# First block: rounding of the first piece of w_out begun ahead of the second front instead of behind it

## The chip, the cores and the metric

The kernel runs on one core of a Trainium2 chip. The metric is the device time of one execution in microseconds (us). A core has five engines that run side by side, each through its own list of instructions in order: TensorE (PE, matrix products; its weight loads are shown as PEld), VectorE (DVE), ScalarE (ACT), GpSimd (POOL) and SyncE (SP, which here only issues DMAs). They wait for each other through semaphores.

## The reference

The first half is a Fourier mixing: for x of 8 x 3008 x 256, the real part of a two-dimensional transform over the sequence and the feature axis. Its result, as 24064 rows of 256, goes through a two-layer network with a squared Relu between:

```python
def _attn_ref(x):
    X = np.fft.fft(x, axis=1)
    X = np.fft.fft(X, axis=2)
    return X.real.astype(np.float32)

def _moe_ref(x, w_in, w_out):
    h = x @ w_in
    r = np.maximum(h, 0.0)
    g = r * r
    return (g @ w_out).astype(np.float32)
```

`w_in` is 256 x 2048 and `w_out` is 2048 x 256. They arrive as 64-bit floats, since they are scaled by a 64-bit number, and are rounded to 32 bits in the kernel.

## The kernel before, in words

**The work.** The transform along the sequence is done as products with tables of cosines and sines (`dft_ops`, results `Pt`, `Qt` and a row `Et` for each of the 8 batches). The transform along the features is folded into the first layer's weights: `begin_win` multiplies each piece of `w_in` with the feature tables and gives `G1` and `G2`. So the first layer reads `Pt`, `Qt` with `G1`, `G2`.

**Steps.** Hidden features come in NJ = 8 pieces of 256 (two times 128). The columns of a batch come in blocks of up to 251. One step `i` is one piece `j` of one block of one batch. Its *front* (L822 to L840) makes on PE, for both halves, a product with `G1` (L832) and one with `G2` (L833), and on DVE a scaled sum with `Et` (L835), a sum (L837) and a difference (L838). `combine` (L845) puts Relu (L847) and Square (L848) on ACT. The *back* of a step (L863) multiplies with `w_out` and comes two steps later (LAG = 2); in the first block it is the plain form, sixteen matmul passes of L872. From the second block on `combine` also makes sums on POOL (L855 to L858), and the back is L885.

**The weights, in the first block.** The eight pieces of `w_in` and of `w_out` are loaded, rounded and used while the eight steps of the first block run. Rounding 64-bit words is `convert` (L263): DVE takes the exponent (L274) and the mantissa (L279) out of the high words, ACT turns the exponent into a 32-bit scale (L276, L277) and, in the shared form, scales the mantissa (L282). That is the first part, issued by the call itself. Later, `halves` puts the sign and the low words in on DVE (L285, L287), and `product` multiplies mantissa and scale, in the shared form on POOL (L292), else on DVE (L294). A load is two DMAs from SP (L259). `load_wout(j, shared)` (L326) is load and first part for a piece of `w_out`; `begin_win(j)` (L300) is the same for a piece of `w_in`, and keeps two more closures: `products` (L305: matmuls L309 with the feature tables, then two copies into `G1`, `G2` on ACT, L310) and `for_e` (L313: four small matmuls L318 with `G2`, then L320 on DVE into `gE`).

**The order.** The program is written out by hand: each engine does its instructions in the order in which the Python code issues them, with no scheduler. In the main loop (L1164), step `i` of the first block issues in this order: `multiply` (the POOL products put off so far), `front`, `weights()` (L1124), `combine`, the back of step i - 2, then `for_e` of the next piece, `leftover` (L1154: `halves` of what lies in `late`) and L320. In `weights()`, step `i` first issues the products of piece i + 1 of `w_in`. Step 0 then begins piece 3 of `w_in`, rounds piece 2 and takes `halves` of piece 3. Step i > 0 loads piece i - 1 of `w_out`, finishes rounding piece i + 2 of `w_in` (not in step 1) and begins piece i + 3 of `w_in`. Piece 0 of `w_out` is so begun in step 1, behind the second front, and read by the first back, in step 2.

The scratch tiles of the rounding rotate in pools: the exponents in two buffers (`fd`), the mantissas in three (`scratch`, L247), the loaded words over several pools (`load`, L251).

Of the kernel before, what the change touches and what calls it, by code (L numbers as in the profile page):

```python
# [82 lines left out]
def kernel(  # L83
# [20 lines left out]
    NJ = NFC // 2  # L104
# [126 lines left out]
    def pair_in(j):  # L231

        return moe_w_in.rearrange("(c p) (h j f) -> j c p h f", p=P, j=NJ, h=2)[j]

    def pair_out(j):

        return moe_w_out.rearrange("(c j p) (o e) -> j c p o e", j=NJ, p=P, o=1)[j]

    def parts(w, k):
        return w.rearrange("p c (e h) -> p h (c e)", h=k)  # L240
# [10 lines left out]
    def load(src):  # L251

        nonlocal raws
        pool, tag = (gp, "g") if raws in (1, 2) else (xp, "x") if raws % (NX + 1) else (ep, "c")
        raws += 1
        single = src.dtype == F32
        raw = pool.tile([P, 2, CH, 1 if single else 2], src.dtype if single else U32, name="raw", tag=tag)
        for c in range(2):
            nc.sync.dma_start(out=raw[:, c].rearrange("p (o e) w -> p o (e w)", o=src.shape[2]),  # L259
                              in_=src[c] if single else src[c].bitcast(U32))  # L260
        return raw

    def convert(dst, raw, shared=False):  # L263


        k = dst.shape[1]
        if raw.dtype == F32:
            return (lambda: None), (lambda: nc.vector.tensor_copy(dst, parts(raw[:, :, :, 0], k))), False
        low, high = raw[:, :, :, 0], raw[:, :, :, 1]
        m = scratch()  # L270
        e = fp.tile([P, 2, CH], F32, name="fd", tag="fd")
        mb, eb = m.bitcast(U32), e.bitcast(U32)

        nc.vector.tensor_scalar(out=eb, in0=high, scalar1=20, scalar2=0x7FF,  # L274
                                op0=ALU.logical_shift_right, op1=ALU.bitwise_and)
        act(e, eb, AF.Relu, bias=ramp[:, 0:1], scale=-1.0)  # L276
        act(eb, e, AF.Relu, bias=ramp[:, 1:2], scale=-2.0 ** 23)  # L277

        nc.vector.tensor_scalar(out=mb, in0=high, scalar1=0xFFFFF, scalar2=0x100000,  # L279
                                op0=ALU.bitwise_and, op1=ALU.bitwise_or)  # L280
        if shared:
            act(m, mb, AF.Copy, scale=2.0 ** -20)  # L282

        def halves():
            nc.vector.scalar_tensor_tensor(out=eb, in0=high, scalar=0x80000000, in1=eb,  # L285
                                           op0=ALU.bitwise_and, op1=ALU.bitwise_or)
            nc.vector.scalar_tensor_tensor(out=m, in0=low, scalar=2.0 ** (-52 if shared else -32),  # L287
                                           in1=m if shared else mb, op0=ALU.mult, op1=ALU.add)

        def product():  # L290
            if shared:
                nc.gpsimd.tensor_tensor(out=dst, in0=parts(m, k), in1=parts(e, k), op=ALU.mult)  # L292
            else:
                nc.vector.scalar_tensor_tensor(out=dst, in0=parts(m, k), scalar=2.0 ** -20, in1=parts(e, k),  # L294
                                               op0=ALU.mult, op1=ALU.mult)

        return halves, product, shared


    def begin_win(j, shared=False):  # L300

        w = ep.tile([P, 2, CH], F32, name="win", tag="sB" if j % 2 else "sA")
        finish = convert(parts(w, 1), win.pop(j, None) or load(pair_in(j)), shared)

        def products():  # L305
            for tab, G, nm in ((cosd, G1, "mC"), (sind, G2, "mD")):
                pg = psm.tile([P, CH], F32, name="pg", tag=nm)
                for i in range(2):
                    nc.tensor.matmul(pg, tab[:, i], w[:, i], start=i == 0, stop=i == 1)  # L309
                nc.scalar.copy(G.rearrange("p (h j f) -> j p h f", h=2, j=NJ)[j],  # L310
                               pg.rearrange("p (h f) -> p h f", h=2))

        def for_e():  # L313

            ps = psd.tile([P, CH], F32, name="pe", tag="d")
            for h in range(2):
                fc = j + NJ * h
                nc.tensor.matmul(ps[:, h:h + 1], G2[:, fc * P:(fc + 1) * P], last, start=True, stop=True)  # L318

            return lambda: nc.vector.tensor_scalar_mul(gE[:, j::NJ], ps[:, 0:2], 0.5)  # L320

        win[j] = finish, products, for_e
# [3 lines left out]
    def load_wout(j, shared):  # L326

        return convert(wout[:, j].rearrange("p h c e -> p h (c e)"), load(pair_out(j)), shared)
# [693 lines left out]
    def rounded(j):  # L1022
        halves, product, _ = win[j][0]
        halves()
        product()
# [93 lines left out]
            f()  # L1119
            spent, room = spent + t, room - t  # L1120

    late, products = [], []

    def weights():  # L1124


        if i + 1 < NJ:
            win[i + 1][1]()
        if i == 0:
            begin_win(3, True)  # L1130
            rounded(2)
            split(win[3][0])
        else:
            mine = [load_wout(k, i != NJ - 2 or k == i) for k in OUT.get(i, ())]
            if 1 < i < NJ - 2:
                rounded(i + 2)
            if i + 3 < NJ:
                begin_win(i + 3)
            for pair in mine:
                late.append(pair)  # L1140

    OUT = {i: (i - 1,) for i in range(1, NJ - 2)}
    OUT[NJ - 2] = NJ - 3, NJ - 2
    OUT[NJ - 1] = NJ - 1,

    def split(pair):
        halves, product, shared = pair
        halves()
        if shared:
            products.append(product)  # L1150
        else:
            product()
# [11 lines left out]
    for i in range(len(steps) + LAG + 4):  # L1164
        if i < len(steps):
            b, k0, n, j = steps[i]
            if i == NJ:
                for k in range(NX):
                    load_later(k)
            if NJ <= i < NJ + NL:  # L1170
                load_column(i - NJ)
            if i % per == 0:
                assert not side
                side = ahead(b + 1) if b + 1 < B else []
                spent, pace = 0.0, sum(t for t, _ in side) / sum(share(i + k) for k in range(per - 2))
            multiply()
            g = front(b, k0, n, j, between)
            if i < NJ:
                weights()
                s = combine(n, g, True)  # L1180
            elif i < 2 * NJ:
                if j < 4:
                    sum_wout(slice(j // 2 * (NJ // 2), (j // 2 + 1) * (NJ // 2)), j % 2)
# [79 lines left out]
```

## Time and profile before

| what | value |
|---|---|
| time, median of 3 runs | 1923.56 us (1923.0 to 1924.24) |
| the profiled execution's own time | 1921.07 us |
| its span, first to last instruction | 1919.3 us |
| mean granted PE clock | 0.999 |
| PE, busy share of the span | 99% |
| DVE, POOL, ACT | 75%, 58%, 50% |
| ACT in the first four fortieths of the span | 20%, 70%, 50%, 50% |
| share of the chain that ended last: PE, DVE | 96%, 3% |
| DMA, mean over the span | 36 GB/s (224 and 118 GB/s in the first two fortieths) |

The page is of one execution. A fortieth of the span is 48 us, so the preparation (tables, first transform) fills about the first, and the first block, with all the rounding of weights, most of the second. The "chain that ended last" follows back from the last instruction, at each step to what released it. A busy time of PE counts matmuls with modelled ends. An instruction's idle time before it is shown in brackets in the timeline, with the engine and line that ended it.

### The profile page before, as it was taken

What the parts mean: (1) busy time and instruction counts of PE and PEld (TensorE: products, weight loads), DVE (VectorE), ACT (ScalarE), POOL (GpSimd) and SP (SyncE); (2) the same over time, 40 slices, a digit from 0 to 9 for tenths busy, and PEclk for the clock granted to TensorE, in tenths of its full rate; (3) what the DMA queues carried; (4) which work ended last, traced back from release to release, by engine and by line L of the source; (5) the groups of instructions that cost most, each with busy time, mean ns of one, the idle gap of its engine ahead of it and who ended that gap; (6) DMA issues with size and microseconds to landing.
All of it is one profiled execution on the core that took longest, in us unless ns stands there. A gap on an engine that the chain in (4) does not pass through costs nothing.

```text
span 1919.3 us, 28162 instructions
## 1 busy us (share of the span) xinstructions
PE 1907.5 (99%) x9270; PEld 1700.7 (89%) x9270; DVE 1444.5 (75%) x3646; ACT 952.4 (50%) x1201; POOL 1120.8 (58%) x1709
## 2 busy tenths in 40 slices
PE   9999999999999999999999999999999999999998
PEld 7888898888988898888988889888898888988887
DVE  8988887787687876788668876788767777655554
ACT  2755554555454554445544454455544555444444
POOL 0255655665566665665566665556655665566565
PEclk9999999999999999999999999999999999999999
DMA  7331211110011101111011100111001101000100
GB/s 224 118 36 30 55 29 36 28 43 16 28 36 42 34 12 35 31 44 28 12 36 44 39 20 12 47 37 36 22 19 45 36 12 22 28 12 12 22 11 23
DMA packets 146622, 69.58 MB, mean 36 GB/s; under 512 B 130145, under 2 KB 137259, under 8 KB 146474
## 3 DMA queue, kind: packets, MB, share of 16 engines
q1 hardware_dynamic: 146022, 66.87, 13.8%
q8 instruction: 73, 1.20, 0.2%
q14 instruction: 75, 0.61, 0.1%
q0 software_dynamic: 176, 0.65, 0.1%
q10 hardware_dynamic: 276, 0.26, 0.0%
HBM read 43.03 MB, written 24.69 MB: 35 GB/s over the span
## 4 chain that ended last, share of the span: by engine, by line
PE 96%; DVE 3%; ACT 0%; DMA 0%; issue 0%; POOL 0%; DVEq 0%; ACTq 0%
PE ph L832 17%; PE ph L833 17%; PE mC L885 16%; PE mA L885 16%; PE mB L885 16%; PE mD L885 8%; PE pd L734 1%; PE pd L626 1%; PE mA L872 1%; PE mB L872 1%; PE pd L708 1%; DMA xt<-in_x_dram 0%; PE pg L309 0%; DVE w L509 0%; DVE fs L479 0%
## 5 line engine op out<-in xcount | busy, mean ns | idle before, releaser
L847 ACT ACTIVATE g<-g 128x1004 f32<-128x1004 f32 (+1 forms) x384 | 399.0, 1039 | 691.8 <-DVE g L838 438.1
L835 DVE SCALAR_TENSOR_TENSOR he<-Et,gE,ph 128x251 f32<-128x251 f32 (+1 forms) x768 | 362.7, 472 | 343.3 <-PE ph L833 338.9
L855 POOL TENSOR_TENSOR s<-g 128x251 f32<-128x251 f32 (+1 forms) x376 | 236.7, 629 | 636.7 <-ACT g L848 578.0
L832 PE MATMUL ph<-Pt,G 128*128 128x251 f32 (+1 forms) x1536 | 452.5, 376 | 0.0
L833 PE MATMUL ph<-Qt,G 127*128 127x251 f32 (+1 forms) x1536 | 451.4, 375 | 0.0
L848 ACT ACTIVATE g<-g 128x1004 f32<-128x1004 f32 (+1 forms) x384 | 399.3, 1040 | 12.2
L885 PE MATMUL mC<-s,wsum 128*128 128x251 f32 (+1 forms) x1504 | 381.5, 375 | 0.0
L885 PE MATMUL mA<-g,wout 128*128 128x251 f32 (+1 forms) x1504 | 380.2, 374 | 0.0
L837 DVE TENSOR_TENSOR g<-he,ph 128x251 f32<-128x251 f32 (+1 forms) x768 | 320.4, 417 | 53.5 <-POOL s L855 1.4
L833 PEld LDWEIGHTS ph<-Qt,G 127*128 127x128 f32 x1536 | 291.6, 190 | 35.4
L885 PEld LDWEIGHTS mC<-s,wsum 128*128 128x128 f32 x1504 | 285.8, 190 | 34.2
L832 PEld LDWEIGHTS ph<-Pt,G 128*128 128x128 f32 x1536 | 285.9, 189 | 33.5 <-DVE he L835 0.2
L838 DVE TENSOR_TENSOR g<-he,ph 128x251 f32<-128x251 f32 (+1 forms) x768 | 314.2, 409 | 0.0
L885 PEld LDWEIGHTS mA<-g,wout 128*128 128x128 f32 x1504 | 283.0, 189 | 34.9 <-issue 0.3
L856 POOL TENSOR_TENSOR s<-s,g 128x251 f32<-128x251 f32 (+1 forms) x376 | 270.7, 720 | 29.5
L857 POOL TENSOR_TENSOR s<-g 128x251 f32<-128x251 f32 (+1 forms) x376 | 272.3, 724 | 0.0
L858 POOL TENSOR_TENSOR s<-g,s 128x251 f32<-128x251 f32 (+1 forms) x376 | 241.8, 643 | 0.0
L885 PE MATMUL mB<-g,wsum 128*128 128x251 f32 (+1 forms) x752 | 220.5, 374 | 0.0
L885 PE MATMUL mD<-s,wout 128*128 128x251 f32 (+1 forms) x752 | 220.4, 374 | 0.0
L885 PE MATMUL mB<-s,wout 128*128 128x251 f32 (+1 forms) x752 | 220.0, 374 | 0.0
L885 PEld LDWEIGHTS mB<-g,wsum 128*128 128x128 f32 x752 | 142.8, 190 | 17.2
L885 PEld LDWEIGHTS mD<-s,wout 128*128 128x128 f32 x752 | 142.1, 189 | 17.5
(176 smaller groups left out, 1386.0 us busy)
## 6 DMA issues: line engine op xcount, KB each, us to landing
out_dram<-os SPq DMA_DIRECT2D x376, 56.0 KB
xt<-in_x_dram SPq DMA_DIRECT2D x39, 384.0 KB
xt<-in_x_dram SPq DMA_DIRECT2D x63, 128.0 KB
Et<-e_dram SPq DMA_DIRECT2D x7, 752.5 KB
out_dram<-os SPq DMA_DIRECT2D x288, 6.8 KB
raw<-in_moe_w_in_dram SPq DMA_DIRECT2D x16, 256.0 KB
raw<-in_moe_w_out_dram SPq DMA_DIRECT2D x16, 256.0 KB
xt<-in_x_dram SPq DMA_DIRECT2D x2, 512.0 KB
```

The lines of the kernel that those rows point to most:

```text
L832: nc.tensor.matmul(hP, G1[:, fs], pt[:, ks], start=True, stop=True)
L833: nc.tensor.matmul(hQ, G2[0:P - 1, fs], qt[0:P - 1, ks], start=True, stop=True)
L835: nc.vector.scalar_tensor_tensor(out=t, in0=et[:, ks], scalar=gE[:, fc:fc + 1], in1=hP, op0=ALU.mult, op1=ALU.add)
L837: tt(out=g[:, h, 0, 0:n], in0=t, in1=hQ, op=ALU.add)
L838: tt(out=g[:, h, 1, 0:n][:, ::-1], in0=t, in1=hQ, op=ALU.subtract)
L847: act(v, v, AF.Relu)
L848: act(v, v, AF.Square)
L855: gt(out=s1, in0=g21, in1=g22, op=ALU.add)
L856: gt(out=s2, in0=s1, in1=g11, op=ALU.subtract)
L857: gt(out=s3, in0=g11, in1=g21, op=ALU.subtract)
L858: gt(out=s4, in0=g12, in1=s2, op=ALU.subtract)
L885: nc.tensor.matmul(acc[nm][:, i, 0:n], w, v[:, 0:n], start=j == 0 and i == 0, stop=j == NJ - 1, skip_group_check=True)
```

## The change

`load_wout(0)` is called at the end of step 0's `weights()` instead of in step 1's. It is kept in `early`, and step 1 only moves it to `late`, so that its second part comes where it came before. Step 1 still begins piece 4 of `w_in` (there is no other load between the two, so the loads keep their order). The rest rewrites the same conditions: `OUT` begins at 2, and `1 < i` is implied.

```diff
-    late, products = [], []
+    early, late, products = [], [], []
...
             begin_win(3, True)
             rounded(2)
             split(win[3][0])
+            early.append(load_wout(0, True))
+        elif i == 1:
+            begin_win(4)
+            late.append(early.pop())
         else:
-            mine = [load_wout(k, i != NJ - 2 or k == i) for k in OUT.get(i, ())]
-            if 1 < i < NJ - 2:
+            mine = [load_wout(k, i != NJ - 2 or k == i) for k in OUT[i]]
+            if i < NJ - 2:
                 rounded(i + 2)
             if i + 3 < NJ:
                 begin_win(i + 3)
-            for pair in mine:
-                late.append(pair)
-
-    OUT = {i: (i - 1,) for i in range(1, NJ - 2)}
+            late.extend(mine)
+
+    OUT = {i: (i - 1,) for i in range(2, NJ - 2)}
     OUT[NJ - 2] = NJ - 3, NJ - 2
     OUT[NJ - 1] = NJ - 1,
```

On the engines, this puts L274 and L279 of piece 0 of `w_out` ahead of L320 and the second front on DVE, and L276, L277 and L282 of that piece ahead of Relu and Square of step 0 and the two copies L310 of piece 2 of `w_in` on ACT. The order on PE, POOL and SP is as before.

## The prediction

> **What bounds the kernel now.** I read the page's busy times first, then the waits of PE alone, then the timeline around the change. The page says that PE is busy for 99% of the span:
>
> ```profile
> PE 1907.5 (99%) x9270; PEld 1700.7 (89%) x9270; DVE 1444.5 (75%) x3646; ACT 952.4 (50%) x1201; POOL 1120.8 (58%) x1709
> ```
>
> A busy PE need not be PE at its best, so the waits of PE over the whole span say more. Their columns are total us, times, longest:
>
> ```profile
> PE mA L872 <- POOL wout L292: 1.9, 1, 1.9
> PE pe L810 <- DVE Qt L663: 1.5, 1, 1.5
> ...
> PE pe L318 <- ACT G L310: 0.9, 2, 0.5
> ...
> PE po L935 <- DVE c L913: 0.5, 1, 0.5
> ```
>
> The two large ones lie in the first 60 us, and after L872's wait PE waits once more in 1862 us, 0.5 us in the last store. So the end moves by as much as PE's stream moves at about 57 us: nothing behind it has slack in which a delay could vanish, and only PE's own stalls of 40 to 57 us can be won. The change works exactly there. The timeline of that stretch (start, duration, engine, instruction; in brackets the idle time before it and who ended it), cut to what the steps use:
>
> ```profile
> 48.93 0.68 DVE L287 SCALAR_TENSOR_TENSOR m<-raw,m 128x512 f32<-128x512 uint32 x1
> 49.16 1.04 ACT L848 ACTIVATE g<-g 128x1004 f32<-128x1004 f32 x1
> ...
> 49.50 1.03 PE L309 MATMUL pg<-win,sind 128*128 128x256 f32 x4
> 49.54 0.15 DVE L320 TENSOR_SCALAR gE<-pe 128x2 f32<-128x2 f32 x1
> ...
> 50.10 0.83 ACT L310 COPY G<-pg 128x256 f32<-128x256 f32 x2
> ...
> 50.99 0.61 PE L318 MATMUL pe<-ident,G 128*128 128x1 f32 x4 [0.46 <-ACT G L310]
> ...
> 52.13 0.42 DVE L274 TENSOR_SCALAR fd<-raw 128x512 uint32<-128x512 uint32 x1
> ...
> 52.59 0.72 ACT L276 ACTIVATE fd<-fd,ramp 128x512 f32<-128x512 uint32 x1 [1.66 <-DVE fd L274]
> ...
> 54.10 1.03 PE L309 MATMUL pg<-win,sind 128*128 128x256 f32 x4
> ...
> 55.48 1.51 POOL L292 TENSOR_TENSOR wout<-m,fd 128x512 f32<-128x512 f32 x1 [4.43 <-DVE gE L320]
> ...
> 57.04 0.69 PE L872 MATMUL mA<-g,wout 128*128 128x251 f32 x2 [1.91 <-POOL wout L292]
> ```
>
> Two things are to be seen. PE stands 1.91 us before 57.04 for the rounded w_out piece 0, whose rounding DVE begins at 52.13. And at 50.99 PE follows ACT by 0.06 us: ACT's two copies of G (50.10, ended 50.93) are already the last thing that the third front waits for. ACT has no slack there.
>
> [...] at 52.59 ACT stood 1.66 us for DVE's L274 with Relu, Square and copies behind it in the list waiting too. The forecast goes by this.
> [...] L228's products (windows: length, PE busy and count, PEld, clock, DMA, GB/s) come at half pace first:
>
> ```profile
> 1.00:5.00 4.00, 3.63 (x17) 3.63 (x18) 1.00 0.80 217
> 5.00:9.00 4.00, 4.00 (x38) 4.00 (x38) 1.00 1.03 295
> ```
>
> That is about 3.6 us of half pace from the first product at 1.37 (the clock column shows no event yet). At the end the last products (L885) are over at 1913.01 and the granted clock is 0.50 from 1916.5 on, 3.5 us later, though eight transposes lie between. In the middle PE is never idle for more than 1.91 us, and the clock is 1.00 throughout. So 1.9 us of idleness is safe here, 3.5 us is not; this is used in step 4.
>
> **The change part by part.** Loads, arithmetic and instruction counts are the same. In the changed program PE, POOL and SP keep their order; the two loads stay where they were on SP (issued at 35.65, and the DMA engines are nearly silent at 43 to 45 us, share 0.06 and 0.04, so the data is there long before). What moves is one pair on DVE (L274, L279) and one triple on ACT (L276, L277, L282).
>
> 1. DVE. The pair goes from 52.13 to behind L287, so it starts at 49.54 in place of L320. It takes 52.13 to 52.80 = 0.67 us, so the second front runs 0.67 us later (L320 at 50.21) and the next pair (piece 4 of w_in) starts at 52.80 as before. The waits that it gains (scratch last read by the rounding ended at 48.41, loads) are over by then. Price on DVE: nothing in sum, 0.67 us for the second front.
>
> 2. ACT. The triple now stands ahead of Relu and Square of step 0 (L847 at 48.10, L848) and of the copies L310. ACT is free at 48.19 but must wait for L274: 49.54 + 0.42 + 0.04 (the latter as from 52.55 to 52.59) = 50.00. The spacings of the timeline are 0.76 (L276 to L277), 0.63 (to L282), 0.52 (to the next), 1.06 (L847 to L848), 0.94 (to L310): so L277 50.76, L282 51.39, L847 51.91, L848 52.97, L310 53.91. Two copies that need not wait take 0.63 (57.87), end 54.54, and PE's L318 follows 0.06 later: 54.60 instead of 50.99, **+3.61 us**. [...]
>
> 3. PE. From L318 to L309's second half is 3.11 us (50.99 to 54.10), so that starts at 57.71, and L872 follows after 0.87 us if nothing holds it (63.55 to 64.42): 58.58. The piece is there: DVE's L285 need no longer wait for ACT and starts at 53.48, L287 at 54.09, POOL 0.76 later (54.72 to 55.48) at 54.85, ended 56.36. So the 1.91 us of waiting is gone and L872 is at 58.58 instead of 57.04: **+1.54 us**. Late next is nothing: the other engines move by less than PE. DVE's third front waits for PE (L835 at about 56.25 instead of 55.57) and is 0.7 us later, which widens POOL's margin ahead of the second L872 (0.24 us now, 62.67 + 1.51 = 64.18 against 64.42) to about 1.1 us.
>
> 4. Clock. In step 2 PE is idle from 50.53 (49.50 + 1.03) to 54.60, 4.07 us. That is beyond the 3.5 us of the kernel's end. If the clock falls, PE starts at half pace, for about 3.4 us as at the beginning; half of it is lost: 1.7. [...] No stretch of the trace has such a gap amid work, so the bounds are 0 (it holds) and 2.8 (restored a window late, below); I take **+1.6**. In that stretch PE is what all wait for, so it lies on the path.
>
> Sum: 1.54 + 1.6 = +3.1 us. The profiled execution took 1921.07 us around its span of 1919.3, so the sum gives 1924.2 (span 1922.4). The median of the runs shown, 1923.56, is 2.5 above the profiled time; with the same distance the forecast is **1926.7**.
>
> **The rivals.**
> *The clock holds.* [...] Against it: 3.5 us sufficed at the end. Then +1.54: 1925.1.
> *The clock comes back one window late: slower by over 0.2%.* Place: the restart at 54.60. [...] Half pace for 4.8 to 5.5 us loses 2.4 to 2.8, with 1.54 about 4.2 us: 1927.8. [...] Against it: a window in the trace at 39.15 to 42.56 was 45% idle and the clock held.
> *The wait is simply removed.* If ACT lost nothing, PE would gain at most the 1.91 us: 1921.7. Against it: ACT cannot start the triple before DVE's 49.54, and the copies stand behind it. DVE's margin is not the matter, ACT's is.
>
> **How the numbers follow.** About 0.2% (3.8 us) is what a measurement of this kernel can tell from no change. Chances: the forecast (clock falls, back after one window) 0.55, clock holds 0.25, clock late 0.13, plain gain 0.03, anything else 0.04. Slower by over 0.2% is nearly all of the late case, the upper edge of the likeliest and half of the rest: 0.17; faster by over 0.2% only by accident: 0.01; within 0.2%: 0.82. The likeliest case's own range is 1925.8 to 1927.4. The range 1924.6 to 1928.2 takes in the clock at both bounds and leaves out the plain gain and the edges.
>
> **What would show it.** Step 1: L274 of the w_out piece at 49.5. Step 2: ACT idle from 48.2 to 50.0 for it, copies L310 at 53.9, PE's L318 at 54.6 with an idle time near 4 us and ACT as releaser. Step 3: no wait of L872 for POOL. Step 4: a clock below 1.00 between 53 and 60 us, products there twice as long. The forecast is wrong if L318 stays near 51, or if PE shows waits behind 60 us that it has not now.

## The result and the profile after

| | before | after |
|---|---|---|
| time, median of 22 runs each | 1922.7 us (1920.27 to 1924.24) | 1925.95 us (1924.04 to 1927.41) |
| ratio | | 1.0017, 95% interval 1.0011 to 1.0024 |
| span of the profiled execution | 1919.3 us | 1922.3 us |
| mean granted PE clock | 0.999 | 0.998 |

The changed kernel is 3.25 us (0.17%) slower. The forecast was 1926.7 us, 3.1 us above 1923.56 us, the median of the three runs shown ahead of it. The median of 22 runs is 0.86 us lower, so the time came out 0.75 us below the forecast, and the difference slightly above it.

Runs of one kernel differ by some 4 us, and some of that lies ahead of the change: the L318 of step 0 starts between 46.0 and 48.8 us in the profiles of this study. From that instruction on the three profiles of the kernel before repeat to a few hundredths. So all profiles are compared from it: the start of step 0's L318 is zero in the table below. Spans are read to 0.1 us, so an end in that table is good to about 0.05 us.

The waits of PE in the changed kernel, whole span (total us, times, longest):

```profile
PE pe L318 <- ACT G L310: 4.6, 2, 4.1
PE pe L810 <- DVE Qt L663: 1.5, 1, 1.5
PE filled L228 <- POOL ident masks.py:199: 1.4, 1, 1.4
PE po L935 <- DVE c L913: 0.5, 1, 0.5
```

The old wait of L872 is gone. L318, which stood 0.5 us for ACT's copies, now stands 4.1 us for them. The timeline of the changed kernel says why:

```profile
49.42 0.42 DVE L274 TENSOR_SCALAR fd<-raw 128x512 uint32<-128x512 uint32 x1
...
49.66 1.31 POOL L292 TENSOR_TENSOR win<-m,fd 128x512 f32<-128x512 f32 x1 [4.00 <-PE pg L309]
49.75 1.49 DVE L279 TENSOR_SCALAR m<-raw 128x512 uint32<-128x512 uint32 x1
49.87 0.72 ACT L276 ACTIVATE fd<-fd,ramp 128x512 f32<-128x512 uint32 x1 [1.80 <-DVE fd L274]
...
51.17 0.15 DVE L320 TENSOR_SCALAR gE<-pe 128x2 f32<-128x2 f32 x1
...
51.82 1.02 ACT L847 ACTIVATE g<-g 128x1004 f32<-128x1004 f32 x1
...
53.82 0.63 ACT L310 COPY G<-pg 128x256 f32<-128x256 f32 x2
...
54.50 0.61 PE L318 MATMUL pe<-ident,G 128*128 128x1 f32 x4 [4.09 <-ACT G L310]
...
55.80 1.52 POOL L292 TENSOR_TENSOR wout<-m,fd 128x512 f32<-128x512 f32 x1 [4.84 <-DVE gE L320]
...
60.16 0.59 PE L872 MATMUL mA<-g,wout 128*128 128x251 f32 x2
```

ACT stands 1.80 us for DVE's L274, does its three, then Relu and Square of step 0, and only then the copies. L872 has no wait in brackets any more: its piece was ready at 57.32. The clock in the same execution (length, PE busy and count, granted clock, DMA share, GB/s):

```profile
54.00:56.00 2.00, 1.50 (x7) 0.83 0.00 0
56.00:58.00 2.00, 2.00 (x6) 0.50 0.54 143
58.00:60.00 2.00, 2.00 (x9) 0.82 0.31 119
60.00:62.00 2.00, 2.00 (x11) 1.00 0.00 0
```

PE is at half clock from 55.3 to 58.7: six matmul records in 2 us where eleven fit at full clock.

### The profile page after: what moved, and what is told of

It reads as the page before. It is cut to its first block, busy times and chain, and to the rows that moved or that the text cites. A ratio compares the mean times of both kernels' runs of the same rounds, so it can differ in the third digit from the quotient of the medians.

```text
span 1922.3 us, 28162 instructions
## 1 busy us (share of the span) xinstructions
PE 1909.7 (99%) x9270; PEld 1701.4 (89%) x9270; DVE 1446.5 (75%) x3646; ACT 953.1 (50%) x1201; POOL 1122.5 (58%) x1709
## 4 chain that ended last, share of the span: by engine, by line
PE 97%; DVE 1%; ACT 1%; issue 0%; DMA 0%; POOL 0%; DVEq 0%; ACTq 0%; POOLq 0%
PE ph L832 17%; PE ph L833 17%; PE mC L885 16%; PE mA L885 16%; PE mB L885 16%; PE mD L885 8%; PE pd L626 2%; PE pd L734 1%; PE filled L228 1%; PE mB L872 1%; PE mA L872 1%; PE pd L708 1%; PE pg L309 1%; DVE he L835 0%; DMA xt<-in_x_dram 0%
## 5 line engine op out<-in xcount | busy, mean ns | idle before, releaser
L832 PE MATMUL ph<-Pt,G 128*128 128x251 f32 (+1 forms) x1536 | 453.0, 376 | 0.0
L837 DVE TENSOR_TENSOR g<-he,ph 128x251 f32<-128x251 f32 (+1 forms) x768 | 320.5, 417 | 53.5 <-POOL s L855 1.4
L832 PEld LDWEIGHTS ph<-Pt,G 128*128 128x128 f32 x1536 | 285.9, 189 | 33.9 <-DVE pd L750 0.2
L838 DVE TENSOR_TENSOR g<-he,ph 128x251 f32<-128x251 f32 (+1 forms) x768 | 314.1, 409 | 0.0
```

The source lines that it names most:

```text
L832: nc.tensor.matmul(hP, G1[:, fs], pt[:, ks], start=True, stop=True)
L837: tt(out=g[:, h, 0, 0:n], in0=t, in1=hQ, op=ALU.add)
L838: tt(out=g[:, h, 1, 0:n][:, ::-1], in0=t, in1=hQ, op=ALU.subtract)
```

## The experiments

Positions in us from the start of step 0's L318; "end" is the end of the span. The last column is the ratio of timed runs to those of before on the same chip, with its interval.

| kernel | L318 of step 1 | first L872 | end | end against before | ratio |
|---|---|---|---|---|---|
| before (three profiles) | 4.64 | 10.69 to 10.70 | 1872.93 to 1872.97 | | |
| changed | 8.27 | 13.93 | 1876.07 | +3.12 | 1.0017 (1.0011 to 1.0024) |
| changed, second | 8.27 | 14.66 | 1876.76 | +3.81 | 1.0020 (1.0013 to 1.0026) |
| changed, third | 8.28 | 15.06 | 1877.20 | +4.25 | single runs: 1925.04 against 1921.29 us |
| gap filled | 8.28 | 12.26 | 1874.37 | +1.42 | 1.0005 (0.9996 to 1.0013) |
| DVE's half alone | 4.64 | 11.60 | 1873.71 | +0.76 | 1.0000 (0.9992 to 1.0008) |
| no first wait | 4.64 | 8.62 | 1872.86 | -0.09 | 0.9994 (0.9986 to 1.0002) |
| behind Relu and Square | 6.31 | 12.03 | 1874.21 | +1.26 | 1.0007 (0.9999 to 1.0015) |
| pair earlier | 7.16 | 12.81 | 1874.94 | +1.99 | 1.0008 (1.0001 to 1.0014) |
| apart | 4.64 | 10.19 | 1872.41 | -0.54 | 0.9995 (0.9987 to 1.0003) |
| halves first | 4.64 | 9.63 | 1876.22 | +3.27 | 1.0014 (1.0007 to 1.0020) |

**The gap filled.** The changed kernel, in step 1 ahead of `for_e`:

```diff
         if i < NJ:
+            if i == 1:
+                idle = psd.tile([P, CH], F32, name="idle", tag="d")
+                for _ in range(16):
+                    nc.tensor.matmul(idle[:, 0:P], ident, ident, start=True, stop=True)
             copy_e = win[i + 1][2]() if i + 1 < NJ else None
```

> The changed kernel with 16 idle products of the identity put on PE into its 4.1 us gap, ahead of L318 of step 1; nothing else moves. Theory (ACT's hold costs about 3.5 us at L318, of which 1.9 come back as the old wait of L872, and the clock that falls in the gap costs a further 1.7): the clock stays at 1.00, L318 still starts at 54.5, L872 at about 58.5, span 1920.8 us, 1.5 above before and 1.5 to 1.7 below the changed kernel. Rival (the gap alone makes the 3 us, the clock's fall lies beside a wait): span 1922.3 as in the changed kernel.

The timeline of PE in this kernel:

```profile
52.04 3.73 PE L1200 MATMUL idle<-ident 128*128 128x128 f32 x32
56.31 0.60 PE L318 MATMUL pe<-ident,G 128*128 128x1 f32 x4 [0.53 <-ACT G L310]
...
60.29 0.59 PE L872 MATMUL mA<-g,wout 128*128 128x251 f32 x2
```

The clock is 1.00 in every stretch up to 100 us, and its mean over the span 1.000. L318 is as late as in the changed kernel (8.28), so ACT's hold is the same; L872 is at 12.26, 1.67 us earlier than with the gap, and the end 1.70 us. That difference is the price of the clock, measured by itself: in the changed kernel the clock was at half from 55.3 to 58.7, 3.4 us, and half of that is 1.7. What is left, +1.42, is ACT's hold less the old wait. The span in the answer to the expectation (1922.4 against 1920.8) is later only because this execution reached step 0's L318 at 48.03. The theory holds.

**DVE's half alone.** ACT's part of `convert` can be put off (`hold`) and is run in step 1 behind the copies:

```diff
-    def convert(dst, raw, shared=False):
+    def convert(dst, raw, shared=False, hold=None):
...
-        act(e, eb, AF.Relu, bias=ramp[:, 0:1], scale=-1.0)
-        act(eb, e, AF.Relu, bias=ramp[:, 1:2], scale=-2.0 ** 23)
+        relus = lambda: (act(e, eb, AF.Relu, bias=ramp[:, 0:1], scale=-1.0),
+                         act(eb, e, AF.Relu, bias=ramp[:, 1:2], scale=-2.0 ** 23))
...
-        if shared:
-            act(m, mb, AF.Copy, scale=2.0 ** -20)
+        scale = lambda: shared and (
+            act(m, mb, AF.Copy, scale=2.0 ** -20))
+        hold.append(lambda: (relus(), scale())) if hold is not None else (relus(), scale())
...
-            early.append(load_wout(0, True))
+            early.append(load_wout(0, True, held))
         elif i == 1:
+            held.pop()()
             begin_win(4)
```

> Only DVE's half of the change: L274 and L279 of piece 0 of w_out ahead of the second front, but ACT's three (L276, L277, L282) back behind the copies L310. Theory (ACT's order makes the price): copies at 50.0, L318 at 50.9, clock 1.00, no gap; L279 is stretched beside POOL as in the changed kernel, so POOL's rounding ends near 57.3 and L872 starts 0.3 to 0.4 us later than before: span 1919.6 us. Rival (the price comes from the delay of the second front on DVE): span 1921 to 1922.3 us.

L318 is back at 4.64: the 4.1 us gap is ACT's order and nothing else. But the end is +0.76, not 0.3 to 0.4. The rival's cause, the late second front on DVE, is at work too, with a smaller effect than the rival gave it; and the clock fell, which the theory had ruled out. The timeline:

```profile
51.23 0.61 PE L318 MATMUL pe<-ident,G 128*128 128x1 f32 x4 [0.46 <-ACT G L310]
53.10 1.21 PE L832 MATMUL ph<-Pt,G 128*128 128x251 f32 x2 [1.26 <-DVE g L838]
```

The third front waits for DVE to give back the PSUM tile of the second. DVE's second front comes 1.75 us late, since L279 takes 1.49 us. And the clock fell at about 52.9, after a gap of 0.46 us and near the end of the one of 1.26, with only the four small products L318 between them. Part of both delays is made up because the old wait of 1.91 us is gone: L872 shows none.

**No first wait.** In the kernel before, in `back`:

```diff
-                        nc.tensor.matmul(acc[nm][:, h, 0:n], wout[:, j, h, c], g[:, c, side, 0:n],
+                        nc.tensor.matmul(acc[nm][:, h, 0:n], wout[:, j, h, c] if j else ident, g[:, c, side, 0:n],
```

> The kernel before, but the first back multiplies with the identity instead of piece 0 of w_out, so that it has no rounding to wait for (the output lacks that piece). It shows what the removed wait of 1.9 us is worth. Theory: next to nothing, since the second back waits for piece 1, which POOL has at 64.2 when the second L872 now starts at 64.4: gain 0.2 to 0.3 us, span 1919.1, with a new wait of about 1.7 us at the second L872. Rival (the wait is a plain loss): gain 1.9 us, span 1917.4.

Of PE's waits, the first line is:

```profile
PE mA L872 <- POOL wout L292: 1.5, 1, 1.5
```

It is the second L872 now: the first starts 2.07 us earlier, and at 63.92 the next stands 1.53 us for the next piece. The end gains 0.09 us. So in these profiles, with the clock at 1.00 around it, the wait that the change removes was worth a tenth of a microsecond: an earlier PE only waits one step later, for the next piece.

**Behind Relu and Square.** ACT's three between step 0's activations and the copies, put off with the same `hold`; the cut shows where they now run:

```diff
     def weights():
...
+        if held:
+            held.pop()()
         if i + 1 < NJ:
             win[i + 1][1]()
```

> The changed kernel with ACT's three instructions behind Relu and Square of step 0 but still ahead of the copies L310 (DVE as in the changed kernel). ACT no longer stands idle; the copies are late by the three alone, 1.9 us. Theory: L318 1.7 us later than before (at 6.3 us behind the L318 of step 0 instead of 4.6), gap 2.2 us, L872 limited by POOL's rounding, 0.3 to 0.5 us later than before: span plus 0.4 us if the clock holds, plus 1.3 if it falls in the gap as it did with DVE's half alone. Rival (delay of the copies passes on one to one, without the old wait in return): plus 1.7 us, or 3.4 with the clock.

L318 at 6.31 is as worked out, the end is +1.26, the value with a falling clock. It fell at about 55.3, when PE had been at work again for almost 2 us, and came back at 58.7. The rival, one to one without any return, is out: with the clock fallen it asked for +3.4.

**Pair earlier.** In the changed kernel the two last lines of step 0's branch change places:

```diff
             rounded(2)
-            split(win[3][0])
             early.append(load_wout(0, True))
+            split(win[3][0])
```

> The changed kernel with DVE's pair (L274, L279 of piece 0 of w_out) one place earlier, ahead of L285 and L287 of piece 3 of w_in, so not beside POOL's L292. Theory: L279 takes 0.42 us instead of 1.49; ACT begins its three 1.2 us earlier, so L318 comes 2.4 us later than before instead of 3.5, gap 2.9 us, and L872 0.3 us later than before: plus 0.3 us if the clock holds, up to plus 2.0 if it falls. Rival (L279's stretch is its own and not POOL's): L279 stays at 1.49 and the second front starts 1.6 us late.

L279 at its new place, in the timeline:

```profile
48.91 0.42 DVE L279 TENSOR_SCALAR m<-raw 128x512 uint32<-128x512 uint32 x1
```

It takes 0.42 us, so the stretch belongs to the neighbourhood of POOL's L292. L318 comes 2.52 us late instead of 3.63 (expected 2.4), and the clock falls at 54.4 for 3.4 us, which costs 1.7. The end, +1.99, is that and the 0.3 of the theory, its upper case.

**Apart.** The pair at that earlier place and ACT's three behind the copies, the two edits together.

> What the runs point to: DVE's pair at the earlier place, away from POOL, and ACT's three behind the copies as before. Theory: L318 as before; the second front 0.67 us later on DVE, which L832 of the third front feels by at most 0.4 us; DVE no longer waits 0.54 us for ACT, so POOL's rounding of piece 0 ends 0.6 us earlier and those behind it too; clock 1.00: span 0.5 to 0.6 us below before. Rival (the second back's wait takes all of it, as without the first wait): no change, within 0.1 us.

End -0.54 us, with L318 at 4.64, L832 of the third front waiting 0.31 us for DVE, L872 still waiting 0.62 us, clock 1.00 around the change. The profile shows the gain; the timed runs (0.9995, 0.9987 to 1.0003) cannot tell it from none. It is the best that was found, and it is 0.03%.

**Halves first.** As apart, and in steps 1 to 5 `split` of the w_out piece ahead of `begin_win`:

```diff
         elif i == 1:
             held.pop()()
+            split(early.pop())
             begin_win(4)
-            late.append(early.pop())
...
+            for pair in mine:
+                split(pair)
             if i + 3 < NJ:
                 begin_win(i + 3)
-            late.extend(mine)
```

> As e7_apart, and in each step of the first block L285 and L287 of the w_out piece ahead of L274 and L279 of the next w_in piece. POOL then begins each rounding 0.67 us earlier, but the pair runs beside POOL. If the stretch of L279 comes from POOL: each pair takes 1.1 us more, DVE (busy throughout in these steps) falls behind by about 1 us a step in five steps, PE waits at each L872: span plus 3 to 6 us. If it does not: span 0.6 to 1 us below before.

DVE and POOL in step 1 of this kernel:

```profile
55.27 0.42 DVE L274 TENSOR_SCALAR fd<-raw 128x512 uint32<-128x512 uint32 x1
55.60 1.74 DVE L279 TENSOR_SCALAR m<-raw 128x512 uint32<-128x512 uint32 x1
```

```profile
55.43 1.62 POOL L292 TENSOR_TENSOR wout<-m,fd 128x512 f32<-128x512 f32 x1 [2.45 <-DVE m L287]
```

The first L872 comes at 9.63, the earliest with a real piece. From there each step loses: L279 takes 1.74 us beside POOL, L872 follows L872 at 8.38 us (57.11, 65.49, 73.87) where a PE without waits needs 7.27 (67.43 to 74.70 in the changed kernel), and the end is +3.27. The arrangement of before, with the pair ahead of the halves, keeps such a pair out of POOL's time.

**The clock, in further profiles.** The clock's edges lay differently against the program: its first rise came 3.63 us behind PE's first product in the first profile of the kernel before (5.00, 1.37) and 6.16 in that of the changed one (7.53, 1.37).

> The changed kernel once more, for a second look at its clock and for times on the same chip. Theory: gap of about 4.1 us ahead of L318 again, a stretch of half clock of about 3.4 us behind it or into it (where it begins may differ), span 1921.5 to 1922.5. Rival (the fall of the clock was chance): clock 1.00 throughout, span 1920.8.

> The changed kernel a third time: gap of 4.1 us ahead of L318 and a fall of the clock again, at another place of the gap; restored after one window of 3.4 us or two. Rival (the fall was chance): clock 1.00.

> The kernel before once more, one look at its clock. With the changed kernel's two profiles the clock fell at 55.3 and at 54.0 us, with half of the change and with the three behind Relu and Square in gaps of 1.3 to 2.1 us. If the windows run freely, the gaps of the kernel before (1.5 us ahead of L810, 1.9 us ahead of L872) should let it fall in some executions: a stretch of 3.4 us at half clock in 40 to 62 us. Theory of free windows: seen in one or both of these two looks. Rival (gaps below 2 us are safe): clock 1.00 in both.

> The kernel before a third time, for the same question: a fall of the clock in its gaps of 1.5 and 1.9 us by the free windows, none by the rival.

The gap is 4.1 us in all three profiles of the changed kernel, and the clock fell each time, at another place. In the second it fell at 54.0 and was back only at 60.8:

```profile
52.00:54.00 2.00, 0.00 (x0) 0.99 0.80 257
54.00:56.00 2.00, 0.19 (x1) 0.50 0.02 5
56.00:58.00 2.00, 2.00 (x7) 0.50 0.00 0
58.00:60.00 2.00, 2.00 (x6) 0.50 0.84 262
60.00:62.00 2.00, 2.00 (x9) 0.80 0.00 0
```

That is 6.8 us, twice the 3.4 of the first. PE worked at half pace from 55.81 on, 5.0 us, losing 2.5; measured against the filled gap, 3.81 - 1.42 = 2.39. In the third it was half from 53.3 to 60.1, with PE at work from 54.38: 5.8 us, half of it 2.9; measured 4.25 - 1.42 = 2.83. So the late return of the clock, a rival of the prediction, is no rare case: it was there in two of three profiles. The two new profiles of the kernel before have the clock at 1.00 in all of their gaps, against the expectation that one would fall.

The timed runs answer that question otherwise, since each has a mean granted clock. In the four profiles that show it (three of the kernel before, the first of the changed one) the half clock at the kernel's end takes at most 3.3 us of the span, which leaves a mean of 0.999 or 1.000. With windows of 3.41 us, the unit in which the clock moved (last section), a mean of 0.998, which needs more than 5.7 us at half clock, means a fall before the end; 0.997 or less needs more than 9.6 us, so two windows or more; 1.000 allows less than 2 us, so no fall of a whole window. By this estimate from those profiles:

- The kernel before lost its clock in at least 24 of 106 timed runs. Their median span is 1921.5 us, against 1919.8 to 1920.0 us for the others. So the fall that was expected does occur. In which gap is not shown. That none of the 60 timed runs of gap filled, no first wait, apart and halves first has 0.998 points at the wait of 1.9 us ahead of L872, which these four lack or have shorter.
- The changed kernel has no timed run of 43 at 1.000, and at least 14 with two windows or more.
- Pair earlier kept its clock in at least 4 of 21 runs (median span 1920.0 us, against 1922.3 us for the 16 at 0.998), DVE's half alone in at least 7 of 13. A fall in the one profile of such a kernel is a case, not the rule.

## Why the prediction was right, point by point

**What bounds.** Right for a delay: no kernel shows new waits of PE after the first block, and in the changed kernel L872 came 3.24 us later and the end 3.12. Not so for a gain: without the first wait, L872 came 2.07 us earlier and the end 0.09.

**Step 1, DVE.** The place was right, a size wrong. The pair was to take 0.67 us; it takes 1.75 (L274 at 49.42 to L320 at 51.17), because L279 stands beside POOL's L292 and takes 1.49 us instead of 0.42. In the profile of before, POOL's L292 already stood where the pair was to go:

```profile
49.77 1.27 POOL L292 TENSOR_TENSOR win<-m,fd 128x512 f32<-128x512 f32 x1 [4.00 <-DVE gE L320]
...
52.47 0.42 DVE L279 TENSOR_SCALAR m<-raw 128x512 uint32<-128x512 uint32 x1
```

So the overlap could have been seen, though not its price. The consequence, a later second front and no price, held only because ACT holds PE for longer; with DVE's half alone PE waits 1.26 us for it.

**Step 2, ACT.** Right in each number: L318 8.27 us behind that of step 0, against 4.64; 3.63 measured, 3.61 forecast. What made it computable is the order on ACT that the trace of before shows: it stood 1.66 us for DVE's L274 and began nothing behind L276 meanwhile. So it was in the changed kernel: Relu of step 0, which begins at 48.10 in the trace of before, begins at 51.82, behind 1.80 us of standing and 1.9 us of work. Moved instructions delayed all behind them by their waiting too.

**Step 3, the old wait.** Right in the sum: +1.54 forecast, +1.42 measured with the gap filled. POOL's rounding came 0.4 us later than before and 1.1 us later than worked out (step 1), which nothing felt. What the forecast did not say is how little the wait was worth by itself, 0.09 us with the clock held. "The wait is simply removed" put an upper limit of 1.91 us on the gain; the run without it shows that the second back would have taken the rest.

**Step 4, the clock.** Right in kind, and in size for the first profile: +1.6 forecast, 1.70 measured (3.12 - 1.42). The half pace at the beginning, to which it refers, is 3.6 us in the trace of before (1.37 to 5.00); the changed kernel's first profile had 3.4. Wrong in two points of its reasoning. "1.9 us of idleness is safe here" does not hold: the clock fell with gaps of 1.3 and 2.1 us in two experiments, and the kernel before itself lost it in at least 24 of 106 timed runs. And the late return had 0.13 of the chance. The 4.8 to 5.5 us of half pace from which its 1927.8 comes were shown by no trace of before; the late return itself showed in two profiles of three, with 5.0 and 5.8 us of half pace, and in at least 14 of 43 timed runs. Between the fall and PE's restart lay 1.85 and 1.06 us. The "clock holds" case had 0.25 and was not seen in the changed kernel. The timed median, +3.25 us, lies between the two cases. That it comes so close to +3.1 is in part luck: the late returns, held too rare, lengthen some of the runs after, and the falls in the kernel before, held impossible, some of those it is compared with.

**The rivals.** That the wait is a plain gain was excluded for the right reason: ACT cannot begin before DVE's L274, and the copies stand behind it.

## What to carry to other kernels

Before an instruction is issued earlier, look on each engine of its chain at what is then behind it, and count the time for which the engine stands as well as the work: here 1.8 us of standing and 1.9 us of work on ACT cost PE more than the wait that was to go. A wait on the bounding engine is worth only what the next wait leaves of it (here 0.09 of 1.91 us); leave the operand out once and see what comes. And a gap on PE has a second price, the clock. Here it fell in gaps between 1.3 and 4.1 us, for the shorter ones in some executions and not in others, so one profile does not tell; the price can be measured by filling the gap with idle products.

## What the runs showed of the hardware

**PE's clock.** The granted clock of the kernel before rises for the first time at 5.00 us and falls at 1916.47. That of the changed kernel, in its first profile, rises at 7.53, falls at 55.31, rises at 58.73 and falls at 1918.99. The stretches between these edges are 560, 14, 1 and 545 times 3.413 us, here called windows. In the five other profiles with a fall around the change the half clock lasted one window (52.9 to 56.3 with DVE's half alone, 55.3 to 58.7 with the three behind Relu and Square, 54.4 to 57.8 with the pair earlier) or two (54.0 to 60.8 and 53.3 to 60.1 in the second and third of the changed kernel).

The edges lay differently against the program from one execution to the next. Besides the first rise, the fall shows it: in the three profiles of the changed kernel the fall came 4.9, 2.2 and 3.0 us behind the beginning of the gap. In three profiles it came when PE was at work again: 0.8 us behind PE's restart in the changed kernel (54.50, 55.31), 0.8 us with the pair earlier (53.62, 54.38) and 1.9 us with the three behind Relu and Square (53.40, 55.28).

The window ahead of a fall was not idle throughout: in the changed kernel PE had been idle for 2.6 of the 3.4 us ahead of 55.31; with the three behind Relu and Square for 1.5 of those ahead of 55.28, and for another 0.5 it had only the products L318 of one column each. With L318 left out, PE was at work for at most 1.41 us in the window ahead of each of the six falls around the change. The least work in a window behind which the clock held is 1.89 us in the kernel before (39.14 to 42.55) and 1.89 in the changed one (38.24 to 41.66). At the kernel's end it fell behind windows with 1.27 us of work (before) and 1.77 (changed). These are readings with modelled ends of products; how much work keeps the clock up is not shown.

**DVE beside POOL.** L279, with one source and both ends in SBUF, takes 0.42 us alone (all sixteen of the kernel before) and 1.49 (changed) or 1.74 (halves first) beside POOL's L292, ending 0.3 us after it; POOL's own goes from 1.27 to 1.31, or from 1.51 to 1.62. L837 and L838, which read PSUM, keep 0.42 and 0.41 beside the L292 at 49.77 in the kernel before. Why L279 is stretched and these are not, no run here shows.
